# Dense units ahead of the first exponential run as couples of 64-row halves

## The chip, the cores and the metric

The kernel runs on one core of one Trainium2 chip. The metric is the device time of one execution in microseconds. The engines are TensorE (PE, with its weight loads shown as PEld), VectorE (DVE), ScalarE (ACT), GpSimd (POOL) and SyncE (SP). All transfers between DRAM and the core's SBUF that matter here are issued by SP, in the order of the program.

## The reference, cut to what matters

```python
x = A_x                                                  # 1 x 2048 x 512
mod = (silu(c) @ w_mod).reshape(1, 6, 1, -1)
sa, ca, ga, sb, cb, gb = (mod[:, i] for i in range(6))
h = layernorm(x) * (1 + ca) + sa
qkv = (h @ wqkv).reshape(1, 2048, 3, 32, 16)             # 32 heads of 16
p = softmax(einsum("bhqd,bhkd->bhqk", q, k) * 16 ** -0.5)
x = x + ga * (einsum("bhqk,bhkd->bhqd", p, v).reshape(1, 2048, 512) @ wo)
h = layernorm(x) * (1 + cb) + sb
a = h @ w1 + b1                                          # 512 -> 1792
x = x + gb * ((a * tanh(softplus(a))) @ w2)              # 1792 -> 512
```

Everything is float32.

## The kernel before, in words

Each float32 operand of a dense product is split into a high and a low part, and a product is three products: high by high, high by low, low by high. A dense unit is one bank of PSUM (128 x 512) and 12 products of 512 columns for queries and keys (`qk_unit`), or half a bank and 12 products of 256 columns for values (`v_unit`). This document counts in slots: one product of 512 columns, or two of 256.

The work falls into steps t. From t = -20 to -1 (`t < 0` in `step`) only two kinds of work run: the row maxima of the first groups of heads, and dense units that make queries, keys and values. From t = 0 to 511 runs the long loop: scores, exponentials (`score`, ScalarE writes `pr`), the maxima of later groups (`max_tile`), the products with the values (`pv`) and half-height dense products beside them (`mm_half`). Steps of the loop are not changed.

In a step with t < 0, `max_pair` makes two pairs of score tiles. A pair is two products over 64 rows each, one in the upper and one in the lower 64 rows of the array, into two neighbouring banks of the PSUM tile `ring`; one VectorE reduction of 128 x 2 x 512 takes the maxima of both. There are 40 pairs; 32 belong to the first group and are closed by `neg_max` (two small reductions into `mm`, a transpose, ScalarE's `mh`, VectorE's `mt`, and four transfers of `mt` into `qa`), 8 to the second. After both pairs of a step, `whole_units` issues 7.2 slots of dense work as products over all 128 rows.

What a dense unit does when its products are done is its `fin`, run one half-step later. For values it is one ScalarE copy into `vq`. For queries and keys it is a ScalarE copy of the bank into `qf` (one buffer), then on POOL `qh`, the high part, and `ql`, the low part (two buffers each), and two half-steps later the put: SP writes `qh` and `ql` to the scratch in DRAM (`qscr`, `kscr`). Later SP loads `qa` and `ka` back from there. Each engine, and SP's queue, runs its instructions in the order of the program, which the Python of the kernel writes out: `at(h, f)` puts an action at half-step h. Half-step numbers are two a step, so -40 is the first.

`plan` lists the dense units: which slice of the weight (0 queries, 1 keys, 2 values), and for which blocks. When the last unit of one entry is done, the weight slice of the entry after next is split (`wh` on ScalarE, `wl` on POOL), and the one after that is loaded (`wr`, SP). `LATE_SPLIT` and `LATE_LOAD` override the half-step of some of these. Beside this, six early weight blocks (`early_prep`, tile `ep`) are loaded, split on POOL and written to `w1scr`, and at half-step 0 SP loads the first parts of the modulation weight (`wm`).

## Time and profile before

| | |
|---|---|
| median of three runs | 1690.04 us (1687.92 to 1691.31) |
| the profiled execution | 1688.32 us, of which the span is 1686.5 us |
| granted clock of TensorE | 0.999 |
| busy over the span | PE 99%, PEld 55%, DVE 85%, ACT 80%, POOL 48% |
| steps with t < 0 | from 47.5 us to 99 us |
| first exponential | 99.62 us |

The page's span runs from the first to the last instruction of the profiled execution; 1.8 us lie around it. A row of the timeline gives the start in us after the span's start, the length, the engine, the line of the kernel, the operation, the tile written and those read, the shape and how many instructions were merged; in square brackets stands how long the engine was idle before and what ended that. SPq rows are SP's issues of transfers; their length is the issue, not the transfer. A row of the busy times gives a stretch, its length, and then busy time and count of each engine, the clock, the DMA engines' busy share and GB/s.

### The profile page before, as it was taken

How to read it: one execution, taken by the hardware profiler on the slowest of the kernel's cores; microseconds unless marked ns; L12 is line 12 of the kernel's file. 1: busy time of each engine (PE TensorE's matmuls, PEld its weight loads, DVE VectorE, ACT ScalarE, POOL GpSimd, SP SyncE). 2: the span in 40 equal slices, each digit the busy share in tenths (PEclk: the TensorE clock that was granted, in tenths of full speed). 3: DMA queues.
4: the chain of work that ended last, by engine and by line, in shares of the span. 5: the costliest groups of instructions: out<-in, count | busy, mean ns of one | idle time of the engine just before them, and what ended most of it. 6: DMA issues, size and time to landing. Idle time of an engine off the chain costs nothing.

```text
span 1686.5 us, 33920 instructions
## 1 busy us (share of the span) xinstructions
PE 1670.4 (99%) x12491; PEld 924.4 (55%) x12491; DVE 1432.9 (85%) x2372; ACT 1357.4 (80%) x2612; POOL 812.5 (48%) x839
## 2 busy tenths in 40 slices
PE   8999999999999999999999999999999999999998
PEld 6755655555445455555555455555555455555687
DVE  6998888888999988888889888888889888883377
ACT  7257777777778988888878998888878988889674
POOL 5555224655313664556323565556323664555442
PEclk9999999999999999999999999999999999999999
DMA  8877656777755334434355434534344433534261
GB/s 261 264 251 188 157 145 197 205 228 218 225 136 161 97 93 104 120 81 130 82 137 161 106 77 98 139 80 122 100 133 120 130 93 81 149 97 135 76 227 63
DMA packets 114983, 239.00 MB, mean 142 GB/s; under 512 B 24500, under 2 KB 50120, under 8 KB 108864
## 3 DMA queue, kind: packets, MB, share of 16 engines
q1 hardware_dynamic: 114808, 236.82, 49.7%
q8 instruction: 99, 1.62, 0.4%
q14 instruction: 68, 0.56, 0.1%
q10 hardware_dynamic: 8, 0.00, 0.0%
HBM read 180.48 MB, written 51.45 MB: 138 GB/s over the span
## 4 chain that ended last, share of the span: by engine, by line
PE 92%; DVE 3%; ACT 2%; DMA 1%; issue 1%; POOL 0%; SPq 0%; ACTq 0%; DVEq 0%; POOLq 0%
PE bk L636 29%; PE ring L618 22%; PE ring L569 19%; PE bk L134 11%; PE bk L127 3%; PE ring L127 2%; PE ring L1249 2%; DVE mx L571 2%; ACT pr L621 1%; PE ring L583 1%; DMA qa<-mt 0%; PE ring L952 0%; PE ring L598 0%; DMA xt<-in_A_x 0%; PE ring L134 0%
## 5 line engine op out<-in xcount | busy, mean ns | idle before, releaser
L571 DVE TENSOR_REDUCE mx<-ring 128x1 f32<-128x512 f32 x1968 | 1221.9, 681 | 150.9 <-PE ring L569 136.2
L621 ACT ACTIVATE pr<-ring 128x512 f32<-128x512 f32 x2048 | 1078.7, 603 | 207.8 <-PE bk L134 116.3
L569 PE MATMUL ring<-ka,qa 64*128 64x512 f32 x1968 | 818.3, 429 | 1.3 <-ACT pr L621 1.0
L618 PE MATMUL ring<-qa,ka 64*128 64x512 f32 x2048 | 759.0, 402 | 3.2 <-ACT pr L621 2.0
L636 PE MATMUL bk<-pr,vg 128*32 128x512 f32 x4096 | 545.1, 604 | 0.0
L569 PEld LDWEIGHTS ring<-ka,qa 64*128 64x128 f32 x1968 | 350.6, 184 | 326.4 <-DVE mx L571 251.4
L618 PEld LDWEIGHTS ring<-qa,ka 64*128 64x128 f32 x2048 | 373.6, 184 | 192.2 <-DVE mx L571 113.3
L134 PE MATMUL bk<-h,w 64*128 64x512 f32 (+1 forms) x1080 | 277.8, 390 | 0.0
L134 PE MATMUL bk<-w,a_h 64*128 64x512 f32 x632 | 210.8, 413 | 0.0
L134 PEld LDWEIGHTS bk<-h,w 64*128 64x128 f32 x1080 | 178.5, 184 | 9.2 <-ACT pr L621 1.5
L636 PEld LDWEIGHTS bk<-pr,vg 128*32 128x32 f32 x4096 | 81.2, 108 | 135.8 <-issue 126.5
L134 PE MATMUL bk<-w,a_l 64*128 64x512 f32 x316 | 124.0, 392 | 0.0
L134 PEld LDWEIGHTS bk<-w,a_h 64*128 64x128 f32 x632 | 106.7, 184 | 3.4 <-ACT hb L830 0.8
L1008 POOL TENSOR_TENSOR y<-yd,y 128x512 f32<-128x512 f32 x44 | 56.8, 1292 | 88.9 <-ACT yd L1007 79.5
L842 POOL TENSOR_SCALAR qq<-ee 128x512 f32<-128x512 f32 x25 | 15.5, 620 | 169.3 <-ACT ee L836 169.3
L858 POOL TENSOR_TENSOR qq<-qq,rr 128x512 f32<-128x512 f32 x42 | 54.1, 1289 | 85.8 <-ACT rr L852 85.8
L844 POOL TENSOR_TENSOR hb<-hb,ee 128x512 f32<-128x512 f32 x42 | 54.1, 1288 | 79.6 <-DVE ee L840 77.6
L134 PE MATMUL bk<-w,o_hl 64*128 64x512 f32 x288 | 79.3, 405 | 0.0
L96 POOL TENSOR_TENSOR a_l<-hb,a_h 128x512 fp32r<-128x512 f32 x53 | 73.1, 1379 | 4.4
L134 PEld LDWEIGHTS bk<-w,a_l 64*128 64x128 f32 x316 | 58.3, 184 | 2.8
L93 POOL TENSOR_SCALAR qh<-qf 128x512 fp32r<-128x512 f32 x27 | 16.7, 620 | 88.3 <-ACT qf L258 68.1
L134 PE MATMUL bk<-h_h,wl 64*128 64x512 f32 x168 | 57.3, 421 | 0.2 <-ACT pr L621 0.2
(222 smaller groups left out, 1901.3 us busy)
## 6 DMA issues: line engine op xcount, KB each, us to landing
ka<-kscr SPq DMA_DIRECT2D x124, 384.0 KB
w<-w2scr SPq DMA_DIRECT2D x56, 512.0 KB
w<-w1scr SPq DMA_DIRECT2D x46, 512.0 KB
vg<-vscr SPq DMA_DIRECT2D x32, 552.0 KB
qa<-qscr SPq DMA_DIRECT2D x124, 100.0 KB
kscr<-qh SPq DMA_DIRECT2D x16, 512.0 KB
qscr<-qh SPq DMA_DIRECT2D x32, 256.0 KB
w2scr<-hl SPq DMA_DIRECT2D x14, 512.0 KB
```

What stands on the lines that cost most here:

```text
L96: (nc.gpsimd if eng == "p" else nc.vector).tensor_sub(lo, src, hi.bitcast(F32))
L127: nc.tensor.matmul(acc, l, r, start=start, stop=stop)
L134: i = nc.tensor.matmul(acc, l[64 * g:64 * g + 64], r[64 * g:64 * g + 64], start=start and not then, stop=bool(stop and then))
L569: nc.tensor.matmul(pm, qt[64 * s:64 * s + 64, qs * P:(qs + 1) * P], kt[64 * s:64 * s + 64, kb * TB:(kb + 1) * TB], start=True, stop=True)
L571: nc.vector.tensor_reduce(out=mxs[n][:, s, 4 * j + qs, kb:kb + 1], in_=pm, op=ALU.max, axis=AX.X)
L618: nc.tensor.matmul(p_, kt[64 * s:64 * s + 64, kc * P:(kc + 1) * P], qt[64 * s:64 * s + 64, :], start=True, stop=True)
L621: e = nc.scalar.activation(pr, p_, AF.Exp, scale=SCALE)
L636: nc.tensor.matmul(accs[n][32 * h:32 * h + 32, :], vgs[n][:, o:o + 32], pts.pop((t, h)), start=(kc == 0), stop=(kc == 15))
L844: (nc.vector if tail else nc.gpsimd).tensor_mul(hb, hb, ee)
L858: nc.gpsimd.tensor_mul(qq, qq, rr)
L1008: nc.gpsimd.tensor_add(y[i], yd, y[i])
L1249: nc.tensor.matmul(po[i // 2][:, i % 2, :], l[:, s], w[:, r, :], start=(f == 0 and j == 0), stop=(f == FT - 1 and j == 2))
```

## The change: what it does

- In steps with t < 0 the dense work is put into couples. A couple is two banks of 12 slots each. Each slot is cut into its upper and lower 64 rows. In the first pass, bank A takes its upper halves and bank B its lower ones, side by side; in the second pass they are crossed over. Both passes have 12 couples of halves.
- The passes of two couples are woven: first pass of one, first of the other, second of one, second of the other. Six couples make 144 slots. The banks ("beds") are the last two of `ring`, and `ms` and `acc`; until the loop begins, the maxima have the first four banks of `ring` instead of six.
- After each pair of maxima (not after two) three or four couples of halves are issued.
- The second pass may add to a bank only after the first pass has written it. Where a first pass has ended, the next `max_pair` gets a ScalarE copy of two columns (`seen`), and the second pass waits for that copy.
- The query unit stands first in `plan`, ahead of the twelve value units; one late split and one late load are no longer overridden.
- All units of a couple are finished together, after the couple's second pass.
- The search for instructions that touch other banks of `ring` looks 96 instructions back, not 32.

With q for the query unit, v4 to v15 for the value units, k10 to k13 for the units of key slice 1 and k20 for the first of key slice 2, the order lists the couples as (q, v4 v5), (v6 v7, v8 v9), (v10 v11, v12 v13), (v14 v15, k10), (k11, k12), (k13, k20).

```diff
-    CREDIT = 7.2
-    LATE_SPLIT = {3: -8, 4: 4}
-    LATE_LOAD = {3: -15, 4: -4, 5: 9}
+    LATE_SPLIT = {4: 4}
+    LATE_LOAD = {4: -4, 5: 9}
...
-        b = ring_at[0] % NRING
+        b = ring_at[0] % ring_of[0]
...
-                for j, b, others, theirs in seen[-32:]:
+                for j, b, others, theirs in seen[-96:]:
...
         nc.vector.tensor_reduce(out=mxs[n][:, :, jq, kb:kb + 1], in_=pm, op=ALU.max, axis=AX.X)
+        if waiting:
+            seen = ap.tile([P, 2], F32, tag="seen", name="seen", bufs=2)
+            e = nc.scalar.copy(seen, pm[:, :, 0])
+            for c in waiting:
+                c["after"] = e
+            waiting.clear()
...
+    COUPLES = 6
+    now, waiting = [0], []
+    beds = [ring_t[:, NRING - 2, :], ring_t[:, NRING - 1, :], "ms", "acc"]
+
+    def lanes():
+
+        def take():
+            bed = bank(beds[0])
+            beds.append(beds.pop(0))
+            slots, fins = [], []
+            while len(slots) < 12:
+                while not units or now[0] < units[0][0]():
+                    yield None
+                half = len(fins) * TB // 2
+                unit = units.pop(0)[1]
+                fins.append(unit(bed[:, half:]))
+                n = 2 if pe_queue[0][0].shape[-1] <= TB // 2 else 1
+                ms = [(*m[:3], m[3] and half == 0, m[4] and len(slots) * n + len(pe_queue) == 12 * n) for m in pe_queue]
+                slots += [ms[j:j + n] for j in range(0, len(ms), n)]
+                pe_queue.clear()
+            return slots, fins
...
+        def turn(c, p):
+            (a, fa), (b, fb) = c["two"]
+            for j, both in enumerate(zip(a, b)):
+                for k in range(max(len(x) for x in both)):
+                    for x, g in zip(both, (p, 1 - p)):
+                        if k < len(x):
+                            mm_half(x[k], g, c["after"] if p and not j and not k else None, p)
+                yield len(a) - j - 1
+            if not p:
+                waiting.append(c)
+                return
+            for fin in fa + fb:
+                at(now[0] + 1, lambda fin=fin, h=now[0] + 1: fin(h))
+
+        for _ in range(COUPLES // 2):
+            c1 = yield from couple()
+            yield from turn(c1, 0)
+            c2 = yield from couple()
+            yield from turn(c2, 0)
+            yield from turn(c1, 1)
+            yield from turn(c2, 1)
+
+    lane = lanes()
+
+    def dense_slots(h, most):
+
+        now[0] = h
+        for _ in range(most):
+            if not next(lane, 0):
+                return
...
-            if second and tm % 16 == 15:
-                neg_max(tm // 16)
-            run_hooks(2 * t + 1)
+                if i and second and tm % 16 == 15:
+                    neg_max(tm // 16)
+                if not i:
+                    run_hooks(2 * t + 1)
+                dense_slots(2 * t + 1, 3 if (2 * tm + i) % 10 < 4 else 4)
...
-            whole_units(2 * t + 1, CREDIT)
+            if t == -1:
+                for _ in lane:
+                    pass
+                ring_of[0] = NRING
...
-    plan = [(-PRO, 2, 0, range(4, 16)), (-PRO, 0, 1, (0,)), (-PRO, 1, 1, range(NB)), (-PRO, 1, 2, range(NB)),
+    plan = [(-PRO, 0, 1, (0,)), (-PRO, 2, 0, range(4, 16)), (-PRO, 1, 1, range(NB)), (-PRO, 1, 2, range(NB)),
...
+    ring_of[0] = NRING - 2
     for t in range(-PRO, T + 2):
```

What moved is seen in three places. In their rows stand the line, the operation, the tile written and those read, the size, and the semaphores waited for.

First, TensorE at the start of the steps with t < 0, before the change: two pairs of maxima, then seven slots over all 128 rows.

```order
L583 MATMUL ring<-ka_98,qa_100 128x512 [waits DMAHW4_49,DMAHW0_49]
L583 MATMUL ring<-ka_98,qa_100 128x512 [waits DMAHW5_49,DMAHW1_49]
L583 MATMUL ring<-ka_98,qa_100 128x512 x2
L127 MATMUL bk<-wh,h_h 128x256 [waits PE_49]
L127 MATMUL bk<-wh,h_h 128x256 x3
L127 MATMUL bk<-wl,h_h 128x256 x4
L127 MATMUL bk<-wh,h_l 128x256 x4
L127 MATMUL bk<-wh,h_h 128x256 [waits PE_49]
L127 MATMUL bk<-wh,h_h 128x256
L583 MATMUL ring<-ka_98,qa_100 128x512 [waits DVE_49]
```

The same place after the change: one pair, then three couples of halves, the query unit's (512 columns) beside the first value units' (two of 256).

```order
L585 MATMUL ring<-ka_98,qa_100 128x512 [waits DMAHW4_49,DMAHW0_49,DVE_49]
L585 MATMUL ring<-ka_98,qa_100 128x512 [waits DMAHW5_49,DMAHW1_49]
L133 MATMUL ring<-h_h,wh 128x512 [waits Activation_49]
L133 MATMUL ring<-wh,h_h 128x256 x2
L133 MATMUL ring<-h_h,wh 128x512
L133 MATMUL ring<-wh,h_h 128x256 x2
L133 MATMUL ring<-h_h,wh 128x512
L133 MATMUL ring<-wl,h_h 128x256 x2
L585 MATMUL ring<-ka_98,qa_100 128x512 x2
```

The dense products moved from `mm_go` (line 127) to `mm_half` (line 133), into banks of `ring`, and the query unit's came to the front.

Second, ScalarE just ahead of the first exponential (`pr`), before the change. `qf` is the copy of a finished query or key unit, `mh` the row maxima.

```order
L258 COPY qf<-bk 128x512 [waits PE_49,Pool_49]
L258 COPY qf<-bk 128x512 [waits PE_49,Activation_49,Pool_49] x2
L89 CAST wh<-wr 128x512 [waits DMAHW3_49]
L600 ACTIVATE mh<-ring 32x128 [waits DMAHW7_49,DMAHW1_49,PE_49]
L258 COPY qf<-bk 128x512 [waits PE_49,Activation_49,Pool_49] x3
L621 ACTIVATE pr<-ring 128x512 [waits DMAHW5_49,PE_49]
```

The same place after the change.

```order
L260 COPY qf<-bk 128x512 [waits Activation_49,Pool_49]
L88 CAST wh<-wr 128x512 [waits DMAHW0_49]
L590 COPY seen<-ring 128x2 [waits DVE_49,Activation_49]
L608 ACTIVATE mh<-ring 32x128 [waits DMAHW7_49,DMAHW1_49,PE_49]
L590 COPY seen<-ring 128x2 [waits DVE_49,Activation_49]
L260 COPY qf<-ring 128x512 [waits PE_49,Activation_49,Pool_49] x2
L260 COPY qf<-bk 128x512 [waits PE_49,Activation_49,Pool_49] x2
L629 ACTIVATE pr<-ring 128x512 [waits DMAHW6_49,PE_49]
```

Two of the copies moved behind `mh`, so that four stand between `mh` and the first exponential, where three stood, and two `seen` copies came in.

Third, SP's queue at the same place, before the change: from the last two transfers of `mt` to the loads of `wm`.

```order
L607 DMA qa_100<-mt 2x4x128 [waits DMAHW7_49]
L607 DMA qa_101<-mt 2x4x128 [waits DMAHW0_49]
L230 DMA wr<-in_A_wqkv 128x4x128 [waits DMAHW1_49,Pool_49]
L272 DMA kscr<-qh 128x2x512 [waits DMAHW2_49,Pool_49]
L273 DMA kscr<-ql 128x512 [waits DMAHW3_49,Pool_49]
L556 DMA vg<-vscr 128x1104 [waits DMAHW4_49]
L309 DMA qa_103<-qscr 50x512 [waits DMAHW5_49]
L309 DMA qa_103<-qscr 50x512 [waits DMAHW6_49]
L318 DMA ka_701<-kscr 48x2048 [waits DMAHW7_49]
L318 DMA ka_701<-kscr 48x2048 [waits DMAHW0_49]
L730 DMA wm<-in_w_mod 128x4x256 [waits DMAHW1_49]
L730 DMA wm<-in_w_mod 128x4x256 [waits DMAHW2_49]
```

The same place after the change.

```order
L615 DMA qa_101<-mt 2x4x128 [waits DMAHW6_49]
L232 DMA wr<-in_A_wqkv 128x4x128 [waits DMAHW7_49,Pool_49]
L558 DMA vg<-vscr 128x1104 [waits DMAHW0_49]
L311 DMA qa_103<-qscr 50x512 [waits DMAHW1_49]
L311 DMA qa_103<-qscr 50x512 [waits DMAHW2_49]
L320 DMA ka_701<-kscr 48x2048 [waits DMAHW3_49]
L320 DMA ka_701<-kscr 48x2048 [waits DMAHW4_49]
L738 DMA wm<-in_w_mod 128x4x256 [waits DMAHW5_49]
L738 DMA wm<-in_w_mod 128x4x256 [waits DMAHW6_49]
L274 DMA kscr<-qh 128x2x512 [waits DMAHW7_49,Pool_49]
L275 DMA kscr<-ql 128x512 [waits DMAHW0_49,Pool_49]
L274 DMA kscr<-qh 128x2x512 [waits DMAHW1_49,Pool_49]
```

The put of a key unit (`kscr` from `qh` and `ql`) stood between `wr` and `vg`; now no put stands there, and the puts of the last four units follow behind the loads of `wm`.

More of the change, by code (lines that the diff above doesn't have):

```diff
@@ L147, in adaln_block @@
     ring_at = [0]
+    ring_of = [NRING]
     kept = []
@@ L160, in bank @@
     def bank(tag="ms"):
+        if not isinstance(tag, str):
+            return tag
         return ring() if tag == "ring" else ps.tile([P, TB], F32, tag=tag, name="bk", bufs=1)
@@ L1308, in whole_units, with couple @@
                 cur["fin"] = None
+    COUPLES = 6
[17 more added lines that the diff above has]
+            return slots, fins
+        def couple():
+            a = yield from take()
+            b = yield from take()
+            return {"two": (a, b)}
+        def turn(c, p):
[24 more added lines that the diff above has]
+                return
     def maxima(n, u, s, others):
```

## The prediction

> **What bounds the kernel now.** I read the page first, for whether time lost ahead of the long loop can be won back in it, then the busy times of the stage ahead of the first exponential, then each engine there in order of time.
>
> ```profile
> span 1686.5 us, 33920 instructions
> ...
> PE 92%; DVE 3%; ACT 2%; DMA 1%; issue 1%; POOL 0%; SPq 0%; ACTq 0%; DVEq 0%; POOLq 0%
> ```
>
> These are the page's span and its chain by engine. TensorE carries 92% of the chain and the loop has no slack, so whatever the start of the loop gains or loses stands in the end time in full.
>
> ```profile
> 47.50:99.00 51.50, 51.38 (x300) 36.62 (x299) 47.60 (x44) 9.82 (x22) 29.87 (x28) 1.00 0.84 274
> ```
>
> This is the stage's row of the busy times (length, then PE, PE loads, DVE, ACT, POOL, each with its instructions; clock, DMA share, GB/s). TensorE is full, but VectorE is nearly so. In order of time:
>
> ```profile
> 48.83 9.27 DVE L585 TENSOR_REDUCE mx<-ring 128x2 f32<-128x1024 f32 x8
> 59.45 1.22 DVE L585 TENSOR_REDUCE mx<-ring 128x2 f32<-128x1024 f32 x1
> 60.39 0.73 PE L583 MATMUL ring<-ka,qa 64*128 64x512 f32 x4
> 60.94 2.36 DVE L585 TENSOR_REDUCE mx<-ring 128x2 f32<-128x1024 f32 x2 [0.27 <-PE ring L583]
> 61.06 0.74 PE L127 MATMUL bk<-wh,h_h 128*128 128x256 f32 x4
> 62.12 0.64 PE L127 MATMUL bk<-wh,h_l 128*128 128x256 f32 x4
> 62.60 0.40 PE L127 MATMUL bk<-wh,h_h 128*128 128x256 f32 x2
> 62.93 0.73 PE L583 MATMUL ring<-ka,qa 64*128 64x512 f32 x4
> ...
> 94.53 4.84 DVE L585 TENSOR_REDUCE mx<-ring 128x2 f32<-128x1024 f32 x4 [0.54 <-PE ring L583]
> ```
>
> A step of this stage lasts 2.54 us (60.39 to 62.93) and holds two pairs of maxima. Unstarved, reductions follow each other every (9.27 - 1.22) / 7 = 1.15 us, so VectorE needs 2.30 us a step: it waits about 0.24 us a step for TensorE (0.27 in the row at 60.94). The last reduction ends at 99.37, the first exponential starts at 99.62 (row below).
>
> **The change part by part.** TensorE first. Couples of halves run in the loop already:
>
> ```profile
> 102.08 0.39 PE L134 MATMUL bk<-h_h,wh 64*128 64x512 f32 x1
> 102.08 0.39 PE L569 MATMUL ring<-ka,qa 64*128 64x512 f32 x1
> 102.32 0.39 PE L134 MATMUL bk<-h_h,wh 64*128 64x512 f32 x1
> 102.55 0.39 PE L134 MATMUL bk<-h_h,wh 64*128 64x512 f32 x1
> ```
>
> A couple of halves takes (102.55 - 102.08) / 2 = 0.235 us. A whole slot of two 256-column matmuls takes 0.48 / 2 = 0.24 us (four from 62.12 to 62.60). Two passes of half-height couples hold as many couples as there were slots, 144, so the dense work costs the same. What goes is the change of shape: four products of the maxima take 0.67 us (60.39 to 61.06) where two couples would take 0.47, so 0.20 us a step, 4.0 us over 20 steps. TensorE then needs (40 + 144) x 0.235 / 40 = 1.08 us for each pair of maxima and VectorE 1.15: the reductions set the pace. Back to back they would end near 48.8 + 40 x 1.15 + 0.6 (two small steps, below) = 95.5, so at most 99.4 - 95.5 = 3.9 us can be won here.
>
> Ring of four banks and the six added ScalarE copies: such a copy reads a bank after its reduction, and the pair after next waits for it. The nearest row is the 0.27 us copy of the row maxima; behind it VectorE has another pair's 1.15 us. I take 0; if one copy stood behind other ScalarE work it would cost up to 1 us once. The wider search for bank dependencies leaves the loop's order as it was: 0.
>
> Queries first. POOL now does the query unit's split before the second early weight split, and only then the low half of the first key slice.
>
> ```profile
> 63.54 0.62 POOL L93 TENSOR_SCALAR ep<-ep 128x512 fp32r<-128x512 f32 x1 [8.22 <-DMA ep<-in_B_w]
> 64.24 1.29 POOL L96 TENSOR_TENSOR ep<-ep 128x512 fp32r<-128x512 f32 x1
> ```
>
> One such pair of steps takes 1.96 us (63.54 to 65.50, where the next begins at the row's end). Early weight, query, early weight, key slice: 63.54 + 3 x 1.96 + 1.29 = 70.7. TensorE wants that slice in the fourth couple, at the nineteenth pair of maxima, near 48.8 + 17 x 1.15 = 68.4 plus 0.5. It waits about 1.9 us; VectorE has a pair in hand, which hides some 0.4. I take 1.5 us lost, with 0 (the weight lands earlier) and 2.5 as ends. On SP the query unit's three puts move ahead of two loads of early weights; those are only split and put away again, and nothing in the stage waits for them: 0.
>
> The end of the stage. All four last units come out in two bursts, at the end of the fifth and of the sixth couple, and on ScalarE their copies stand directly ahead of the first exponential. Now they are spread out:
>
> ```profile
> 95.49 0.59 ACT L258 COPY qf<-bk 128x512 f32<-128x512 f32 x1 [3.87 <-PE bk L127]
> 96.16 0.62 POOL L93 TENSOR_SCALAR qh<-qf 128x512 fp32r<-128x512 f32 x1 [1.68 <-ACT qf L258]
> 96.87 1.28 POOL L96 TENSOR_TENSOR ql<-qf,qh 128x512 fp32r<-128x512 f32 x1
> 99.13 0.59 ACT L258 COPY qf<-bk 128x512 f32<-128x512 f32 x1 [3.06 <-PE bk L127]
> 99.62 2.07 ACT L621 ACTIVATE pr<-ring 128x512 f32<-128x512 f32 x4
> 100.04 0.62 POOL L93 TENSOR_SCALAR qh<-qf 128x512 fp32r<-128x512 f32 x1 [1.89 <-DMA kscr<-qh]
> 102.31 2.22 ACT L621 ACTIVATE pr<-ring 128x512 f32<-128x512 f32 x4 [0.62 <-PE ring L618]
> ...
> 108.72 1.89 POOL L734 TENSOR_TENSOR wm<-wm,sil 128x1024 f32<-128x1024 f32 x1 [2.32 <-DMA wm<-in_w_mod]
> ```
>
> `qf` has one buffer: copy, high part, low part, next copy is a ring of 98.15 - 95.49 = 2.66 us, 2.7 with the hand-over. `qh` and `ql` have two: the third unit's high part must wait until the first unit's has landed in DRAM, and the row at 100.04 shows such a wait. In the order on SP the first unit's put stood ahead of the loads of `vg`, `qa`, `ka` and `wm`; it now stands behind them.
>
> ```profile
> 88.85 0.34 DVE L592 TENSOR_REDUCE mm<-mx 128x16 f32<-128x64 f32 x2
> 91.38 0.33 DVE L601 SCALAR_TENSOR_TENSOR mt<-mh,lows,ring 32x128 fp32r<-32x128 f32 x1
> 91.77 2.79 SPq L607 DMA_DIRECT2D qa<-mt  x4
> 94.66 0.40 SPq L230 DMA_DIRECT2D wr<-in_A_wqkv  x1
> 95.16 0.45 SPq L272 DMA_DIRECT2D kscr<-qh  x1
> ...
> 99.17 1.62 SPq L730 DMA_DIRECT2D wm<-in_w_mod  x2
> ```
>
> ```profile
> kscr<-qh SPq DMA_DIRECT2D x3, 512.0 KB
> wm<-in_w_mod SPq DMA_DIRECT2D x2, 512.0 KB
> kscr<-ql SPq DMA_DIRECT2D x3, 256.0 KB
> ka<-kscr SPq DMA_DIRECT2D x2, 384.0 KB
> vg<-vscr SPq DMA_DIRECT2D x1, 552.0 KB
> ...
> wr<-in_A_wqkv SPq DMA_DIRECT2D x1, 256.0 KB
> qa<-qscr SPq DMA_DIRECT2D x2, 100.0 KB
> ```
>
> From the issue of `wr` (94.66) to the landing of the first `wm` (108.72, where POOL had waited for it) 14.1 us passed, for 256 + 512 + 256 + 552 + 200 + 768 + 512 = 3056 KB. In the new order the first unit's put is done after 256 + 552 + 200 + 768 + 1024 + 512 = 3312 KB, at that pace 15.2 us after `wr`.
>
> The sum. `mt` ends after 34 reductions: 48.8 + 34 x 1.15 + 0.6 + 1.5 = 90.0 (91.7 now). Then 0.1 + 2.8 + 0.1 to `wr`: 93.0. The put lands at 108.2. High part 0.7, low part 1.3, hand-over 0.05, last copy 0.5 (99.13 to 99.62): the first exponential starts at 110.75, which is 11.1 us later than 99.62. TensorE meanwhile fills the ring and stops. It gets 0.6 us back, because the second four exponentials now wait 0.62 us for it and will find their products made. So +10.5: 1688.3 for the profiled execution becomes 1698.8. The median of the three runs, 1690.0, is 1.7 above that execution, so I say 1700.
>
> [...]
>
> **Rivals.** *The put overtakes the loads.* SP itself needs 100.8 - 94.7 - 1.0 (two puts of some 0.5 us gone) = 5.1 us from `wr` to the end of the `wm` issues, so the put is issued near 98.1. The put issued at 95.16 had landed by 100.04, 4.9 us later. At that latency the new one lands at 103.0, and the first exponential comes at 105.6: +6.0 - 0.6 = +5.4, 1694 to 1695.5. For it: in one queue only the order of issue is seen, not that landings keep it. Against it: the `wm` row, 9.5 us from issue to landing. [...] The rows have only one direct pair of times for it, so it gets 0.16.
>
> *The front is slower too.* Four-slot pairs need 0.235 x 5 = 1.18 us of TensorE against 1.15, with two pairs of banks in place of three. If each of the 24 lost 0.1 us (2.4 us) or the key slice came 2.5 us late, `mt` and all behind it move by 2 to 4 us: 1702 to 1704.5. Against it: 16 pairs with three slots leave 0.2 us each. 0.14.
>
> *The wait never binds (not slower).* One thing decides it: the first unit's put has landed before 98.0, when the third unit's high part is due (TensorE ends couple five 1.2 us after the 35th reduction, at 48.8 + 35 x 1.15 + 0.6 + 1.5 + 1.2 = 92.4; copies every 2.7). Then four chained copies alone put the first exponential at 92.6 + 3 x 2.7 + 0.5 = 101.2, so +1.6 - 0.6 = +1.0: 1691. For it: DMA is not busy when SP comes free of `mt`:
>
> ```profile
> 92.00:96.00 4.00, 4.00 (x20) 2.80 (x19) 3.46 (x4) 0.51 (x1) 2.13 (x3) 1.00 0.30 109
> ```
>
> (DMA share 0.30). Against it: the put is only issued at 98.1. 0.07. That the exponentials come early with the reductions, -3.9 us or 1686, needs the copies to stand aside as well: 0.05.
>
> **How the numbers follow.** Main case 0.58 (1697 to 1702), overtaking 0.16 (1694 to 1695.5), slower front 0.14 (1702 to 1704.5), no binding wait 0.07, gain 0.05. The range 1694 to 1704 holds the first two and most of the third and leaves out the last two. A measurement tells about 0.2% here, 3.4 us: slower 0.88 (the first three), same 0.07, faster 0.05.
>
> **What would show it.** In the changed kernel's trace: reductions in the stage with no idle but one gap of 1 to 2 us near 71; no shape change, products of one pair plus dense halves at 0.235 us; on ScalarE four `qf` copies, the last over 8 us after the third, its release POOL's `ql`; on POOL one `qh` that waits some 8 us for a DMA of `kscr`; the first exponential near 110; the loop's steps as long as before. I am wrong if the third unit's high part starts by 100, or if the loop's steps differ.

## The result, and the profile after

| | before | after |
|---|---|---|
| median of five runs | 1690.0 us (1687.92 to 1691.31) | 1705.51 us (1703.04 to 1707.02) |
| ratio, with its 95% interval | | 1.0093 (1.0078 to 1.0108) |
| the profiled execution | 1688.32 us, span 1686.5 | 1707.02 us, span 1705.2 |
| granted clock of TensorE | 0.999 | 0.992 |
| first exponential | 99.62 us | 111.04 us |

The kernel became slower by 15.5 us where 10 were predicted, and 1705.5 lies above the predicted range. The first exponential stands within 0.3 us of the predicted 110.75. The profiled execution is 18.7 us longer than before's, so another 7 us are missing behind it. The page, its span, the granted clock in 40 slices and the chain by engine:

```profile
span 1705.2 us, 34373 instructions
...
PEclk9979999999999999999999999999999999999999
...
PE 89%; DVE 4%; DMA 3%; ACT 2%; issue 1%; POOL 1%; SPq 0%; ACTq 0%; DVEq 0%; POOLq 0%
```

TensorE's share of the chain fell from 92 to 89%, and the third slice (85 to 128 us) has a lower clock; before, all 40 slices had a 9. Now the place that the prediction spoke of, ScalarE and then GpSimd and SP in order of time:

```profile
97.16 0.59 ACT L260 COPY qf<-ring 128x512 f32<-128x512 f32 x1 [2.12 <-POOL ql L95]
99.84 0.59 ACT L260 COPY qf<-bk 128x512 f32<-128x512 f32 x1 [2.09 <-POOL ql L95]
110.56 0.59 ACT L260 COPY qf<-bk 128x512 f32<-128x512 f32 x1 [10.13 <-POOL ql L95]
111.04 1.58 ACT L629 ACTIVATE pr<-ring 128x512 f32<-128x512 f32 x3
```

```profile
93.76 0.39 SPq L232 DMA_DIRECT2D wr<-in_A_wqkv  x1
97.41 1.10 SPq L274 DMA_DIRECT2D kscr<-qh  x1
...
108.56 0.62 POOL L92 TENSOR_SCALAR qh<-qf 128x512 fp32r<-128x512 f32 x1 [8.76 <-DMA kscr<-qh]
```

The fourth copy comes 10.7 us after the third, because GpSimd's `qh` for k13 waits 8.76 us for k11's put. That put is done 14.8 us after `wr` was issued (108.56 - 93.76). What the sum did not hold is what TensorE does next. Its rows behind the wait, and the busy times of all engines in steps of 4 us (length, then PE, PE loads, DVE, ACT, POOL; granted clock, DMA share, GB/s):

```profile
111.69 0.79 PE L571 MATMUL ring<-ka,qa 64*128 64x512 f32 x1 [10.02 <-ACT pr L629]
...
114.23 0.62 PE L133 MATMUL bk<-h_h,wh 64*128 64x512 f32 x1
...
114.66 0.62 PE L133 MATMUL bk<-h_h,wh 64*128 64x512 f32 x1
```

```profile
104.00:108.00 4.00, 0.00 (x0) 0.00 (x0) 0.00 (x0) 0.00 (x0) 0.00 (x0) 0.50 1.08 376
...
112.00:116.00 4.00, 3.71 (x17) 2.40 (x16) 2.29 (x4) 2.41 (x5) 1.20 (x1) 0.50 0.57 214
116.00:120.00 4.00, 4.00 (x19) 2.63 (x15) 3.05 (x5) 2.69 (x5) 1.72 (x2) 0.55 0.00 0
120.00:124.00 4.00, 4.00 (x33) 1.71 (x32) 3.12 (x6) 3.19 (x7) 3.43 (x3) 1.00 0.40 135
```

While TensorE idles its granted clock falls to 0.50, and it stays there for some 8 us after the work is back: 19 matmuls in the step from 116, 33 in the step from 120. A couple of halves takes 0.43 us (114.23 to 114.66) instead of 0.235. The trace's clock record has one stretch of half clock from 102.5 to 119.6 us. Exponential by exponential against before, the first is 11.42 us late and the 25th 14.13 (130.47 against 116.34). So 2.7 us were lost where the prediction gave 0.6 back.

The rest of this execution's 18.7 us lies far behind:

```profile
394.78 0.46 PE L626 MATMUL ring<-qa,ka 64*128 64x512 f32 x1 [3.76 <-DMA qa<-mt]
```

Once, TensorE waits 3.76 us for a transfer of 4 KB. 3.41 us of half clock follow from 396.1, and the exponentials, late by 14.0 until there, are late by 18.3 afterwards.

### The profile page after: what moved, and what is told of

Read it like the earlier page. It is cut to its first block, busy times and chain, and to the rows that moved or that the text cites. A ratio compares the mean times of both kernels' runs of the same rounds, so it can differ in the third digit from the quotient of the medians.

```text
span 1705.2 us, 34373 instructions
## 1 busy us (share of the span) xinstructions
PE 1670.2 (98%) x12707; PEld 933.0 (55%) x12707; DVE 1433.3 (84%) x2372; ACT 1358.4 (80%) x2618; POOL 812.8 (48%) x839
## 4 chain that ended last, share of the span: by engine, by line
PE 89%; DVE 4%; DMA 3%; ACT 2%; issue 1%; POOL 1%; SPq 0%; ACTq 0%; DVEq 0%; POOLq 0%
PE bk L644 29%; PE ring L626 22%; PE ring L571 19%; PE bk L133 11%; PE ring L1257 2%; PE ring L126 2%; DVE mx L573 2%; ACT pr L629 1%; PE bk L126 1%; DVE mx L587 1%; DMA kscr<-qh 1%; PE ring L133 1%; DMA qa<-mt 1%; PE ring L960 0%; PE ring L606 0%
## 5 line engine op out<-in xcount | busy, mean ns | idle before, releaser
L850 POOL TENSOR_SCALAR qq<-ee 128x512 f32<-128x512 f32 x25 | 15.5, 621 | 168.3 <-ACT ee L844 168.3
L133 PE MATMUL bk<-h_h,wl 64*128 64x512 f32 x192 | 64.2, 429 | 0.9 <-POOL wl L95 0.9
```

The source lines that it names most:

```text
L133: i = nc.tensor.matmul(acc, l[64 * g:64 * g + 64], r[64 * g:64 * g + 64], start=start and not then, stop=bool(stop and then))
```

## The experiments

Each comparison has runs of the kernel before on the same chip: medians 1688.40 (e1 to e4), 1688.62 (e5 to e8), 1688.21 (e9 to e12) and 1688.71 (e13, e14). The table holds every run but e8, which the text gives. "Loss behind" is how much later than before the 25th exponential is, less how much later the first is. "Half clock behind" is the time that the clock record shows at 0.50 between these two.

| | median, us | to before, us | ratio (95% interval) | first exp., us | loss behind, us | half clock behind, us |
|---|---|---|---|---|---|---|
| after, first trace | 1705.51 | +15.5 | 1.0093 (1.0078 to 1.0108) | 111.04 | 2.71 | 8.55 |
| e9, after again | 1704.63 | +16.4 | 1.0095 (1.0081 to 1.0109) | 115.31 | 2.50 | 8.12 |
| e1, own buffers | 1697.65 | +9.3 | 1.0056 (1.0041 to 1.0071) | 106.19 | 1.92 | 6.83 |
| e2, mod loads later | 1701.82 | +13.4 | 1.0080 (1.0065 to 1.0095) | 110.50 | 1.76 | 5.98 |
| e10, put first | 1696.20 | +8.0 | 1.0042 (1.0028 to 1.0055) | 104.91 | 2.42 | 7.93 |
| e3, hold of 12 | 1695.02 | +6.6 | 1.0043 (1.0026 to 1.0060) | 103.50 | 1.76 | 6.07 |
| e4, hold of 24 | 1703.38 | +15.0 | 1.0088 (1.0073 to 1.0103) | 112.80 | 1.77 | 6.35 |
| e12, hold of 24, 60 products | 1705.40 | +17.2 | 1.0097 (1.0082 to 1.0113) | 114.87 | 2.23 | 6.83 |
| e13, hold of 24, 66 products | 1702.29 | +13.6 | 1.0080 (1.0061 to 1.0100) | 114.11 | -0.02 | 0 |
| e5, order alone | 1697.32 | +8.7 | 1.0052 (1.0037 to 1.0067) | 107.99 | -0.01 | 0 |
| e6, cover | 1697.41 | +8.8 | 1.0054 (1.0039 to 1.0069) | 101.68 | 6.64 | 6.83 |
| e7, cover and loads | 1696.77 | +8.2 | 1.0048 (1.0033 to 1.0063) | 102.81 | 5.79 | 3.41 |
| e14, lent tiles | 1691.14 | +2.4 | 1.0015 (1.0005 to 1.0024) | 101.68 | 0.08 | 0 |
| e11, lent tiles, preparations later | 1687.49 | -0.7 | 0.9991 (0.9982 to 1.0000) | 96.41 | 0.92 | 0 |

**The wait for the put.** e1 gives k11 and k12 tiles of their own, so that k13 needn't wait for a put.

```diff
-            qh = qp.tile([P, TB], F32R, tag="qh", name="qh", bufs=2)
-            ql = qp.tile([P, TB], F32R, tag="ql", name="ql", bufs=2)
+            if (kind, ct, tb) in ((1, 1, 1), (1, 1, 2)):
+                qh = ap.tile([P, TB], F32R, tag="p1", name="qh", bufs=4)
+                ql = ap.tile([P, TB], F32R, tag="p3", name="ql", bufs=4)
+            else:
+                qh = qp.tile([P, TB], F32R, tag="qh", name="qh", bufs=2)
+                ql = qp.tile([P, TB], F32R, tag="ql", name="ql", bufs=2)
```

> The changed kernel, but the high and low parts of the two units of couple five (k11, k12) go to buffers of their own, taken from the tiles of the exponentials, so that couple six's parts need not wait for couple five's puts. Theory 1 (the first exponential is held by the landing of couple five's put): no POOL wait for a DMA of kscr of more than 1 us, the four copies 2.7 us apart, the last at about 102.5 us, the first exponential at about 103.0 instead of 111.0, no idle of TensorE over 3 us there; about 8 us off plus what a slowed clock cost (2.7 us): 1693 to 1696. Rival (the couples themselves or the order of units cost the time): the first exponential moves, but the total stays above 1700.

The wait is gone and the four copies are 2.7 us apart, from 97.67 to 105.71, but all of them come 3.2 us later than in the first trace of after, and the first exponential with them. So the time, 1697.65, lies over the 1693 to 1696 expected and under the 1700 of the rival.

```profile
72.69 0.79 PE L133 MATMUL bk<-h_h,wl 64*128 64x512 f32 x1 [2.73 <-POOL wl L95]
...
105.71 0.59 ACT L264 COPY qf<-bk 128x512 f32<-128x512 f32 x1 [2.09 <-POOL ql L95]
106.19 1.59 ACT L633 ACTIVATE pr<-ring 128x512 f32<-128x512 f32 x3
```

TensorE waited 2.73 us for the low half of the first key slice, and ran at half clock until 75.5 behind that. e2 and e10 leave the buffers and take transfers out of the put's way on SP.

```diff
 e2
-                at(max(0, h + 2), lambda: first_mods(max(0, h + 2)))
+                at(max(6, h + 2), lambda: first_mods(max(6, h + 2)))
 e10
-                at(max(0, h + 2), lambda: first_mods(max(0, h + 2)))
+                at(max(4, h + 2), lambda: first_mods(max(4, h + 2)))
-    for pp, h in ((2, -22), (3, -2)):
+    for pp, h in ((2, -22), (3, 2)):
```

> The changed kernel, with the two loads of the modulation weight (1024 KB) issued six half-steps later, behind the puts of couples five and six. Theory 1: the put of k11 lands after 2288 KB instead of 3312 KB; at the 224 KB a us measured (3312 KB from 93.8 to 108.6) that is 10.2 us after the load of wr, near 104; first exponential near 106.5, 4.5 us earlier than in the changed kernel; total 1699 to 1701.5. Rival (a put overtakes loads, or something other than bytes ahead of it holds it): the first exponential does not move by more than 1 us.

> The changed kernel with the loads of the fourth pair and of the modulation moved four half-steps back on SP, behind the puts of k11 and k12: between the load of wr and the end of k11's put stand 256 + 552 + 512 = 1320 KB instead of 3312. If the place in the queue is what made the put late, it lands at 100 to 102, the wait of GpSimd for it is under 2 us, the copies keep their 2.7 us and the first exponential stands at 103 to 104 with a front as in after (106 with the later front of the first two variants); with 1 to 2 us of half clock behind it the time is 1693 to 1697. If a put of scratch takes its 11 us wherever it stands, the wait stays over 6 us and the time over 1700.

GpSimd's `qh` for k13, in e2 and then in e10:

```profile
108.02 0.62 POOL L92 TENSOR_SCALAR qh<-qf 128x512 fp32r<-128x512 f32 x1 [6.74 <-DMA kscr<-qh]
```

```profile
102.42 0.62 POOL L92 TENSOR_SCALAR qh<-qf 128x512 fp32r<-128x512 f32 x1 [0.70 <-ACT qf L260]
```

With 1320 KB between `wr` and the end of the put, the wait is gone and 8.4 us come back (16.4 to 8.0). So the place in SP's queue made the put late, as e10 expected. e2 was missed. At the prediction's pace 1024 KB fewer are worth 4.7 us, and they brought 2.0 (the front, that is the stage up to `mt`, was also 1.5 us later than in the first trace): the put is done 12.8 us after `wr` (95.21) instead of 14.8, 179 KB per us instead of 224. From e2 to e10 only the 968 KB of `qa` and `ka` move out of the way, worth 4.4 us at that pace, and the put is done at least 6.0 us sooner (at most 6.8 us after `wr`, 95.65 to 102.42). So these loads from scratch held the put more than their bytes say, and those of `wm` less. The pace that the prediction took from one pair of rows depends on which transfers are in the queue.

**The clock.** e3 and e4 take the kernel before and add only copies on ScalarE ahead of the first exponential, into a tile that is written again before it is used.

```diff
+    def hold():
+        for _ in range(12):          # 24 in e4
+            nc.scalar.copy(gates[0], ones.to_broadcast([P, D]))
+
+    at(0, hold)
```

> The kernel before, with twelve ScalarE copies (a broadcast constant into a tile that is written again later; about 0.55 us each) put ahead of the first exponential; no other part is changed. It makes TensorE wait without any part of the change: first exponential near 103.2 instead of 99.6, TensorE idle some 3 us. Theory 2 (an idle TensorE comes back at half clock for several us, and that is the part of the loss beyond the late first exponential): the granted clock falls below 1.0 after the gap, and the total rises by 3.6 plus 0 to 3 us. Rival (the rest of the loss belongs to the couples): clock stays 1.0 and the total rises by about 3 us.

> As the one with twelve, with twenty-four copies: first exponential near 109.8, TensorE idle some 9 us. Theory 2: half clock for some 8 to 17 us after the gap, total up by 10.2 - 0.6 + 3.3 = about 13 us, 1703. Rival: clock 1.0, total up by about 9.6 us, 1699.6.

Both lose 1.8 us behind the first exponential, with 6 us of half clock there, and without anything of the change. In e4 the first exponential came 3.0 us later than expected and the loss behind was smaller than the 3.3 expected, so the sum came near 1703 with neither term right. The length of the wait (5.22 us of TensorE in e3, 14.20 in e4) makes no difference. That a half clock stands beside the loss does not yet show that it is the cause, so the next three kept TensorE busy in the wait.

```diff
+        if h == 0:
+            for _ in range(24):
+                nc.scalar.copy(gates[0], ones.to_broadcast([P, D]))
+        if h == 1:                                   # 2, with 48 products, in e8
+            spare = bank("acc")
+            for _ in range(66):                      # 60 in e12
+                nc.tensor.matmul(spare, h_h[:, 0, :P], h_h[:, 0, :TB], start=True, stop=True)
```

> The kernel before with the hold of 24 ScalarE copies again (it adds copies ahead of the first exponentials, and nothing else of the change), and 48 products of 512 columns on TensorE in the stretch in which it would idle (their results are thrown away): about 11 of the 13 us. Without them the hold moved the first exponential by 13.18 us and the loop by 14.94, with 17.07 us of half clock; 1703.4 us. If idling TensorE is what halves its clock, no half clock stands behind 100 us here, the loop moves by 12.5 to 13.2, and the time is 1700.5 to 1701.5. If the clock isn't the reason and a late start of the loop costs 1.8 us more in another way, it is 1703 to 1704 as without the products.

> The kernel before with the hold of 24 ScalarE copies behind the last of its own, and 60 products of 512 columns whose results are thrown away, now at the place in TensorE's order where it stops for the first exponential (in the first try they stood behind that place and ran after the hold). The hold ends near 115.6 as there, +16.0. If idling TensorE is what halves its clock, none shows between 100 and 125 us, the loop moves by as much as the first exponential, 15.5 to 16.2, and the time is 1703.5 to 1705. If the late start costs 1.8 us by another way, the loop moves by 17.5 to 18 and the time is 1706 or more.

> As the kernel before with the hold of 24 copies and 60 thrown-away products, with 66 products: 15.3 us instead of 13.9, to the end of the hold near 114.9, so that TensorE has at most 0.5 us of idle time ahead of the loop. If idle time of TensorE is what halves the clock and so costs the loop about a third of a microsecond for each microsecond at half clock, there is no half clock behind 100 us, the loop moves by what the first exponential moves (15.2 to 15.8) less up to 0.6, and the time is 1703 to 1704.5. If the loop still loses 1.8 us or more after the first exponential, with the clock full, a late start costs something by another way, and the time is 1705 to 1706.5.

e8 tells nothing of the clock: its products stood behind the place where TensorE stops, ran after the hold (12.44 us from 117.42) and made it 1715.93 us (+27.3). e12 came out at neither theory's number. Its products end at 113.4, and a short wait was left (the row of TensorE, and the step of 4 us behind it):

```profile
115.51 0.67 PE L569 MATMUL ring<-ka,qa 64*128 64x512 f32 x1 [1.66 <-ACT pr L621]
```

```profile
116.00:120.00 4.00, 3.71 (x17) 2.45 (x14) 2.60 (x4) 2.22 (x4) 0.00 (x0) 0.50 0.00 0
```

These 1.66 us were enough for 6.83 us of half clock, and the loop lost 2.23 us. e13 closes the gap with six more products:

```profile
98.78 15.25 PE L1549 MATMUL bk<-h_h 128*128 128x512 f32 x66
114.76 0.50 PE L569 MATMUL ring<-ka,qa 64*128 64x512 f32 x1 [0.29 <-ACT pr L621]
```

```profile
116.00:120.00 4.00, 3.55 (x26) 2.48 (x26) 3.57 (x6) 3.34 (x8) 0.42 (x1) 1.00 0.00 0
```

The clock stays at 1.00 (the hold ended 0.8 us earlier than expected, so the time is lower too), and the 25th exponential is late by what the first is, 14.47 and 14.49 us. The same hold with 0.29 us of idle time on TensorE loses nothing behind. As far as the 25th exponential, a late start by itself costs nothing more and gives nothing back. That was tried in the kernel before; in the changed kernel the half clock stands beside the loss. Over the table the loss is 0.28 to 0.33 us for each microsecond of half clock, wherever no other wait stands there (e6 and e7 have one, below; e11's 0.92 come with a wait for a store of `w1`).

**The order alone.** e5 has the changed order of units and the two shorter tables in the kernel before, and no couples.

```diff
-    LATE_SPLIT = {3: -8, 4: 4}
-    LATE_LOAD = {3: -15, 4: -4, 5: 9}
+    LATE_SPLIT = {4: 4}
+    LATE_LOAD = {4: -4, 5: 9}
...
-    plan = [(-PRO, 2, 0, range(4, 16)), (-PRO, 0, 1, (0,)), (-PRO, 1, 1, range(NB)), (-PRO, 1, 2, range(NB)),
+    plan = [(-PRO, 0, 1, (0,)), (-PRO, 2, 0, range(4, 16)), (-PRO, 1, 1, range(NB)), (-PRO, 1, 2, range(NB)),
```

> The kernel before with only the order of the changed one: the query unit ahead of the value units, and the two tables of due times cut down to match; no couples, whole 128-row products, each unit closed by itself. If the loss hangs on the couples closing two units at once, the k11 and k12 copies keep their old spacing here, the put of k11 isn't pushed behind the loads with a unit right after it that needs its buffer, and the time is that of before, 1687 to 1691 (on the chip of the first four experiments before had 1688.4). If the order of the slices alone brought a good part of the loss, by key slices split later, it is 1694 or more.

Missed: it costs 8.7 us. The split of a key slice is now due right behind the query unit, long before the slice has landed, and on ScalarE it stands ahead of the copies of the value units.

```profile
62.11 0.62 ACT L89 CAST wh<-wr 128x512 fp32r<-128x512 f32 x1 [8.86 <-DMA wr<-in_A_wqkv]
```

```profile
63.05 1.22 PE L127 MATMUL bk<-wh,h_h 128*128 128x256 f32 x4 [5.90 <-ACT vq L287]
```

With couples the banks are not asked back so soon: in the first trace of after this split waits 0.87 us (at 62.17) and TensorE doesn't wait there at all, so the 8.7 us are not a part of after's 15.5. For the clock e5 is a second witness: its first exponential is 8.37 us late, TensorE did not idle just ahead of it, and the loss behind is zero.

**After once more.**

> The changed kernel once more, for a second trace of it. If the late transfer of 4 KB near 391 us and the half clock behind it (4.5 us in the first trace) are chance, they may be missing here; then the loop stands at +13.5 to +14.5 to its end and the profiled execution takes about 1703. If they belong to the change, they stand here too, and the profiled execution takes 1706 to 1707. The first exponential is near 111 by every theory, with 10 us of wait for the put of k11 ahead of it.

The late 4 KB are missing here (TensorE waits 0.27 us at that place), so they are not a steady cost of the change. The profiled execution took 1706.07 us all the same, not 1703, because the first exponential came 4.3 us later still. SP's last loads of the maxima's keys, GpSimd's first early weight and the reductions, in the first trace and in this one:

```profile
57.04 1.71 SPq L320 DMA_DIRECT2D ka<-kscr  x4
...
63.03 0.63 POOL L92 TENSOR_SCALAR ep<-ep 128x512 fp32r<-128x512 f32 x1 [9.25 <-DMA ep<-in_B_w]
...
71.70 13.75 DVE L587 TENSOR_REDUCE mx<-ring 128x2 f32<-128x1024 f32 x12 [0.91 <-PE ring L585]
```

```profile
60.16 1.71 SPq L320 DMA_DIRECT2D ka<-kscr  x4
...
66.12 0.63 POOL L92 TENSOR_SCALAR ep<-ep 128x512 fp32r<-128x512 f32 x1 [10.87 <-DMA ep<-in_B_w]
...
75.82 1.23 DVE L587 TENSOR_REDUCE mx<-ring 128x2 f32<-128x1024 f32 x1 [4.71 <-PE ring L585]
```

A load of keys that starts 3.1 us later on SP makes the early weights 3.1 us later, GpSimd's split of the key slice stands behind them, and VectorE loses 4.71 us instead of 0.91. About half of the 3.1 us is a later start of the whole stage (first reduction at 49.52 and 48.05). In e1, e2, e6, e10 and e14 the gap was 3.8, 1.8, 3.2, 3.4 and 2.9 us; the first trace of after had the shortest of them.

VectorE has other gaps in that first trace, which the prediction's sum doesn't hold:

```profile
48.05 1.23 DVE L587 TENSOR_REDUCE mx<-ring 128x2 f32<-128x1024 f32 x1 [0.66 <-PE ring L585]
...
51.46 19.33 DVE L587 TENSOR_REDUCE mx<-ring 128x2 f32<-128x1024 f32 x17 [0.48 <-PE ring L585]
...
86.69 1.23 DVE L587 TENSOR_REDUCE mx<-ring 128x2 f32<-128x1024 f32 x1 [1.24 <-PE ring L585]
```

The first pair of maxima starts after 1.45 us of waiting on TensorE, for VectorE's `ql` that reads `ring` (before, it started without a wait). The ring cut to four banks is the likely reason, but that wasn't tried by itself. Half clock follows from 47.9 to 51.3 and costs the next two reductions 0.47 and 0.48 us. Near 86, TensorE waits 1.30 us for the high part of the second key slice, whose load came late (ScalarE's split at 84.79 waited 3.31 us for it).

**Taking all waits away.** e6 keeps the couples, gives k11 to k20 separate `qf` tiles and k11 and k12 separate `qh` and `ql`, all among the exponentials' tiles (`p0` to `p3`), and puts k20's copy behind the first exponentials. e7 also starts the six early preparations later.

```diff
-            for fin in fa + fb:
-                at(now[0] + 1, lambda fin=fin, h=now[0] + 1: fin(h))
+            for i, fin in enumerate(fa + fb):
+                h = now[0] + 1 + 2 * (now[0] == -1 and i)
+                at(h, lambda fin=fin, h=h: fin(h))
...
 e7
-        at(3 * i - 37, lambda i=i: early_prep(i, 3 * i - 37))
+        at(3 * i - 31, lambda i=i: early_prep(i, 3 * i - 31))
```

> The changed kernel with all couples as they are, but the waits behind the last two couples taken away: qh and ql of k11 and k12 and the four qf in tiles of their own, and the copy of k20 two half-steps later, behind the first exponentials. TensorE closed its last couple at 97.8 us in the profile of after, the first score ended at 98.7. If late copies and the clock that drops behind them are the whole loss, the first exponential stands at 98.8 to 99.5 when the front runs as in after (102 when it stalls near 71 us as in the two variants of the changed kernel so far), no stretch of half clock stands behind 100 us, and the time is 1687 to 1691. If the couples or the new order of products cost the loop something of their own, the time stays over 1693 with the first exponential back at 99.

> As the one before, and the six early preparations of w1 (load, split on GpSimd, put) start six half-steps later, so that GpSimd splits the low part of the first key slice ahead of them instead of behind three of them. In after that split began at 68.92, in the two variants of the changed kernel at 69.5 and 71.4, and VectorE lost 0.91, 1.8 and 3.8 us there. If that is what made the front of those variants late, no gap over 0.5 us stands near 71 us, no half clock there, the last pair of maxima ends at 97 to 98 and the time is 1 to 3 us under the kernel with own buffers alone: 1686 to 1688. If the preparations, later now, meet the second key slice or the first exponentials' buffers instead, the gap moves to 85 to 95 us and the time is no better.

Both times were missed; in e7 what its last sentence allows for came true, that the gap moves and the time is no better. In e6 the front's gap (3.2 us) made the first exponential 2.1 us late, and the tiles were a bad choice: the ninth exponential needs the one that still waits for k11's put. e7 has that wait too (4.04 us). In e7 the gap near 71 is gone and stands at the second key slice instead.

```profile
111.36 1.23 ACT L634 ACTIVATE pr<-ring 128x512 f32<-128x512 f32 x2 [4.20 <-DMA kscr<-qh]
```

```profile
91.63 1.23 DVE L592 TENSOR_REDUCE mx<-ring 128x2 f32<-128x1024 f32 x1 [4.07 <-PE ring L590]
```

e14 keeps k20's copy where e6 has it, and lends k11 to k20 the two output tiles (`o_0`, `o_1`), which nothing uses before the end of the first group of heads. e11 also starts the first four preparations six half-steps later and the last two ten.

```diff
+    def lent(i):
+        if i not in loan:
+            loan[i] = ap.tile([P, DK, TB], F32R, tag=f"o_{i}", name="loan", bufs=1)
+        return loan[i]
...
+            spare = {(1, 1, 1): 0, (1, 1, 2): 1}.get((kind, ct, tb))
+            if spare is not None:
+                qh, ql = (lent(0)[:, 2 * spare + i, :] for i in range(2))
...
+                late = {(1, 1, 1): 0, (1, 1, 2): 1, (1, 1, 3): 2, (1, 2, 0): 3}.get((kind, ct, tb))
+                qf = pw.tile([P, TB], F32, tag="raw", name="qf", bufs=1) if late is None else lent(1)[:, late, :].bitcast(F32)
...
 e11
-        at(3 * i - 37, lambda i=i: early_prep(i, 3 * i - 37))
+        at(3 * i - 31 + 4 * (i > 3), lambda i=i: early_prep(i, 3 * i - 31 + 4 * (i > 3)))
```

> The kernel with lent tiles, without the later start of the preparations of w1: only the waits behind the last couples are gone, the front is that of the changed kernel. If the front's stall near 71 us is a loss by itself, it shows here as a gap of 1 to 5 us of VectorE there, the last pair of maxima ends 1 to 5 us later than with the preparations moved (95.8 there), the first exponential stands at 98 to 102, and the time is 1689 to 1693. If the stall is paid back by slack before the first exponential, the time is 1687 to 1688 as with the preparations moved.

> All waits behind the last couples taken away without the price of the last try: qh, ql and qf of k11 to k20 lie in the two output tiles that nothing uses before the end of the first group of heads, so that no exponential waits for a put (4.2 us in the two kernels that put them among the exponentials' own tiles); the copy of k20 is two half-steps later; the first four preparations of w1 start six half-steps later and the last two ten, so that neither key slice's split stands behind them. If late copies, the stalled front and the halved clock are the whole loss, the last pair of maxima ends at 97 to 98, the first exponential stands at 98 to 99.5, no half clock follows it, and the time is 1686 to 1689, as before or up to 2 us under it. If the couples cost the loop something by themselves, or if the front stalls again at the second key slice, it is 1691 to 1695.

TensorE in e14, then VectorE and ScalarE in e11:

```profile
72.33 0.60 PE L133 MATMUL bk<-h_h,wl 64*128 64x512 f32 x1 [1.98 <-POOL wl L95]
```

```profile
49.23 36.30 DVE L599 TENSOR_REDUCE mx<-ring 128x2 f32<-128x1024 f32 x32 [0.66 <-PE ring L597]
...
96.41 2.06 ACT L641 ACTIVATE pr<-ring 128x512 f32<-128x512 f32 x4 [0.38 <-PE ring L583]
```

In e11 VectorE runs all 32 pairs of the first group without a gap, the last pair ends at 95.79 (99.37 before), and the first exponential starts 3.2 us earlier than before. That is earlier than the 97 to 98 and 98 to 99.5 expected. So the couples do what their cost said. In the time 0.7 us of it is left, with an interval that just reaches no change (0.9982 to 1.0000). Between the 9th and 41st exponential 1.6 us are given up to new short waits (1.21 us behind a store of `w1` at 103.6), and the runs spread from 1685.5 to 1689.6. e14 measures the stalled front, with gap, first exponential and time where it was expected: 2.4 us slower than before, 3.1 more than e11. From e14 to e1 the copies that wait for each other ahead of the first exponential, with the clock behind them, add 6.8 us (2.4 to 9.3), and the wait for the put adds another 7.1 (9.3 to 16.4). These differences cross chips and let the pieces overlap, and the first of them also holds the later copy of k20, so they are sizes, not an exact sum.

## Why the prediction was wrong

The direction and the cause were right, and the chain of waits was found where the prediction put it. The number failed by two terms.

- *"It gets 0.6 us back"* is the step that failed outright. It took TensorE to be at full speed behind a wait of 10 us. The measured term is +2.7 and +2.5 us in the two traces, an error of 3.2 us. e4, e12 and e13 show its cause: behind waits of TensorE of 14.20 us (e4) and 1.66 us (e12) the granted clock stood at 0.50 for 6.35 and 6.83 us of the work behind the first exponential, and 1.77 and 2.23 us were lost; behind one of 0.29 us (e13) it stayed at 1.00 and nothing was lost. The sentence on what would refute it, "or if the loop's steps differ", named this without a price. The trace of before has a half clock too: 3.41 us of it from 23.3 us, behind a wait of TensorE of 1.32 us that ends at 21.44 (the last section has more). The prediction did not weigh that.
- *"I take 1.5 us lost, with 0 and 2.5 as ends"* for the first key slice's split is the term that was mis-sized. It stands for all that VectorE loses between its first reduction and `mt`, and the same stretch measures 3.1 us in the first trace (90.81 - 48.05 - 34 x 1.15 - 0.6) and 5.7 in the second (94.88 - 49.52 - 34 x 1.15 - 0.6). VectorE's gap at the first key slice was 0.91 us in the first trace and 4.71 in the second, and up to 3.8 in the variants. The mechanism was right: early weight, query, early weight, key slice on GpSimd, in that order. But the arrival of the early weight was taken as fixed at 63.54, and it varies (63.03 to 66.12) with a load on SP in front of it. In the second trace the clock is at half beside this gap too (72.2 to 79.1). The rest is the gaps shown above: the half clock at the start of the stage and the late second key slice, which has no term in the sum. *"Ring of four banks ... I take 0"* leaves out the wait of the first pair as well, 0.66 us of VectorE. The rival *the front is slower too*, at 0.14, was nearer to the second trace than the main case.
- *The landing of the put*, 15.2 us after `wr`: 14.8 in the first trace and 15.0 in the second (97.83 to 112.83). The number held, with nearly the same transfers in the queue as in the rows that the pace came from; e2, at 179 KB per us instead of 224, and e10 show that kilobytes over a pace is no law. The rival *the put overtakes the loads* (4.9 us from issue to landing) fell: 11.1 us.
- *The first exponential at 110.75*: 111.04 and 115.31. That the first is so near is luck in part. The stage began 0.8 us earlier than before (48.05 against 48.83), the front lost 1.6 us more than taken, and the put landed 0.4 us sooner behind `wr`. The row maxima's `mt` at 90.0: 90.81 (its row starts at 90.48). Four copies, the last over 8 us after the third: 10.7. No change of shape, couples at 0.235: confirmed by the rows at full clock.
- *"At most 3.9 us can be won here"*: e11 wins 3.6 of it in the reductions. The gain was real and was buried under two waits.
- The single late transfer at 391 us cost the first trace 4.5 us and wasn't foreseen. Since the second trace lacks it, it explains that execution and not the median.

As measured, the first exponential and the loss behind it make +14.1 us in the first trace (11.42 + 2.71) and +18.2 in the second (15.70 + 2.50), where the sum had +10.5. The median's +15.5 lies between them.

## What to carry to other kernels

A wait of TensorE can cost more than its length: ahead of the first exponential, half clock stood behind waits of 1.66 us (e12) to 14.20 us (e4), and none behind 0.29 us (e13). About 0.3 us were lost for each microsecond at half clock (0.28 to 0.33), some 2 us in all here, and the full loop gave nothing of a late start back (-0.02 us behind it in e13), so don't count on that. When units of work are bundled, look at where their closings land: four copies that used to lie apart now stood in a row ahead of the first exponential, on one buffer, and behind one put that had been moved behind 2.5 MB of loads. A term that hangs on the arrival of a transfer needs a second trace, or ends as wide as that arrival varies.

## What the runs showed of the hardware

- The clock record has half clock in stretches of 3.41 us (before, from 23.3; after, from 47.9 and from 396.1), 6.83 us (e12, from 115.7) and 17.07 us (after, from 102.5), and not only behind long waits: gaps of TensorE of 1.66 (e12), 1.73 (e2, at 70.9) and 1.98 us (e14, at 72.3) had 3.41 to 6.83 us of it behind them, gaps of 0.85 (after, at 70.2) and 1.30 us (after, at 85.5) none.
- The length of a gap doesn't decide it alone. A gap of 1.32 us has half clock behind it in before (it ends at 21.44) and none in after (at 20.96). All nine traces with couples have a gap of 1.44 or 1.45 us at the start of the stage. In six of them (after, e1, e2, e6, e10, e14) half clock follows at once, in three (e7, e9, e11) it doesn't: from 48 to 56 us the mean clock is 0.79 in after, e1 and e2, and 1.00 in e9 and e11.
- What decides it was not shown. The traces of before and after can be cut into stretches of 3.41 us on whose edges their clock record changes. From 4 to 1680 us, four of these at full clock have half clock behind them, and TensorE's rows fill 50% of one (before, from 19.9) and 53, 35 and 38% of three (after, from 44.5, 99.1 and 392.7). Of the other 968 at full clock, with full clock behind them, one is filled to 52% (after, from 389.2) and the rest to 61% or more. No run moved a gap against these edges.
- A wait of 14.2 us cost no more clock behind it than one of 5.2: 6.35 and 6.07 us of half clock, 1.77 and 1.76 us of loss (e4, e3).
- In the second trace of after the put of keys to scratch was issued 1.8 us later than in the first, and the next load of keys started 5.8 us after that issue instead of 4.5 (52.58 to 57.04; 54.34 to 60.16). Together that moved GpSimd's early weights by 3.1 us. What makes it vary stays open. The first early weight came at 63.54 us in the kernel before, and at 65.51, 63.66 and 64.96 us in e1, e2 and e6.
